# Packed attention, folded FFT and a two-layer block in seven products: two PSUM tiles instead of one, and down products dealt out between the block products

## The chip, the cores and the metric

The kernel runs on one core of a Trainium2 chip. The metric is device time in microseconds of one execution, as a median over runs. All data is float32.

## The reference

Attention is applied twice with a small set of packed tokens, then a Fourier mixing and a two-layer block:

```python
p_packed = sm_attn(p, k, v)            # B,H,S,D = 8,8,576,64; 32 packed tokens per head
x = sm_attn(q, p_packed, p_packed)     # softmax(scale * q k^T) v, scale = 1/8
x = x.transpose(0, 2, 1, 3).reshape(8, 576, 512)
u = x + np.real(np.fft.fft(np.fft.fft(x, axis=1), axis=2))
un = (u - mean(u)) / sqrt(var(u) + 1e-6)          # over the 512 features
return u + np.maximum(un @ w1, 0) @ w2            # w1 512 x 2048, w2 2048 x 512
```

## The kernel before

**Precision.** Every float32 operand of a large product is held as a high part and a low part (the remainder), both in a rounded format. One product is three matmuls: high·high, high·low, low·high. ScalarE makes a high part by a copy, VectorE or GpSimd the low part by a subtraction (helper `split`, lines 110 and 111).

**Rows and tiles.** The 8 × 576 rows of `u` are 36 groups of 128: four per batch and one of remainders per pair of batches. Four groups make a tile, so there are nine tiles of 512 rows, numbered 0 to 8. For each batch `front(b)` computes attention and the Fourier part and leaves rows of `u` in SBUF. It is a generator: the string ORDER lists its pieces, a `y` in it gives control back, and each call of `step(i)` in the block's code lets it run one stretch further. The front of batch t+1 is spread in this way over tile t. A tile's block (both layers) runs on TensorE between those pieces. The PSUM banks that a front uses come from `bank()`, which deals out a pool of two, and, in the first tiles, accumulators and `pb`.

**Order.** From tile 1 on TensorE, VectorE, ScalarE and GpSimd take their instructions in the order in which the code is written. SP's DMA queue is in order as well: a load that waits for its buffer holds up what is behind it.

**Plain form, tiles 0 and 1 (`ffn`).** There are 16 hidden blocks of 128. `up` makes one block's 512 columns in bank `ph` by 12 matmuls; ScalarE applies relu and VectorE forms the low part; `down` adds 12 matmuls into the accumulators `acc0` to `acc3`. In tile 1 `combine` (line 748 is its GpSimd part) writes, for each pair of hidden blocks, seven combinations of weights to DRAM, of 256 KB each.

**Seven-product form, tiles 2 to 8 (`fast_ffn`).** Two hidden blocks times two halves of the rows are four products of halves, and they are made from seven products instead of eight, eight times a tile; each of these eight is called a step here, m = 0 to 7. The right operands are B11, B21, B22 (quarters of the turned rows, in `uh` and `ul`) and the combinations T1 to T4 (in the tiles `fast`, the high parts in one and the low parts in another). One product is six matmuls of 128 × 256 (line 878), and goes to a half of one of the two PSUM banks `ph` and `pb`. These banks are one tile, `pair`. Four quarters come out as sums: B11 + B21, which collects in one half-bank and goes through relu at L899; `u2` = B11 + T2 (ScalarE copy L893, VectorE add L895); `u3` = `u2` + T3 + T1 (L906, L907), relu L909; and `u2` plus the half-bank that collects T1 and B22, beside `u2` plus that of T3 and T4, both in one 512-wide add (L919), relu L920. L884 makes the low parts on VectorE. Then 24 matmuls of 128 × 512, the downs (L936), add the two hidden blocks into the accumulators. The downs of step m−1 are all issued between T3 and B22 of step m:

```python
begin(m)            # B11, copy, T2, add, T1, B21, relu
step(4 * m - 2)     # a piece of the front
second(m)           # T3 and its sums; then 8 downs of m-1, step, 16 downs
end(m)              # B22, T4, the wide add; then step
```

After step 7 the tile's last 24 downs run at once, and `leave` (L944, L945) adds the accumulators to `u` and stores.

**Pieces and weights.** SP fetches the pieces (L762, one 256 KB piece per product) into a ring of eight slots, which lie in the space that `w1` had. A slot is fetched again as soon as its product has been issued. The `w2` rows are split once per hidden block and tile (L110, L111).

**Turning rows.** `Turned.less` normalises a row group of the next tile (L667), `moves` transposes it on TensorE by four 128 × 128 transposes into a bank (L676), and `parts` makes the high and low parts and T1 to T4 from it. Row groups 0 and 1 are turned in step 7, and 2 and 3 among the last 24 downs.

Of the kernel before, what the change touches and what calls it, by code (L numbers as in the profile page):

```python
# [17 lines left out]
P = 128  # L18
S = 576
# [33 lines left out]
RING = 8  # L53
# [29 lines left out]
def tile_kernel(ctx, tc, kpT, qT, v, w1, w2, tabs, tabR, tabB, tabT, sel, ident_d, out):  # L83
# [12 lines left out]
    pair = psf.tile([P, 2, 512], F32, tag="pair", name="pair")  # L96
    ph, pb = pair[:, 0, :], pair[:, 1, :]
# [556 lines left out]
    class Turned:  # L654
# [25 lines left out]
        def parts(self, i):  # L680
# [19 lines left out]
            nc.gpsimd.tensor_tensor(q[:, 1], raw[:, 2:4, w], r[:, 1], ALU.subtract)  # L700
# [3 lines left out]
            nc.scalar.copy(sh[:, 2:4], q)  # L704
            nc.gpsimd.tensor_tensor(sl[:, 2:4], q, sh[:, 2:4].bitcast(F32), ALU.subtract)
# [10 lines left out]
    def groups():  # L716

        if not fast:
            for i in range(3):
                fast[i] = work.tile([P, GROUPS[i + 1] - GROUPS[i], 512], F32R, tag=f"w1{i}", name=f"fast{i}", bufs=1)  # L720
        return fast

    def mixed():
        return [groups()[i][:, 0:4, :].rearrange("p i (k t) -> p i k t", k=2) for i in (1, 2)]

    def piece(n):
        i, a = ((1, 4), (1, 5), (2, 4), (2, 5), (0, 0), (0, 1), (0, 2), (0, 3))[n % RING]
# [53 lines left out]

    def ffn(first, turned, step, nxt):
# [41 lines left out]
        prev = None  # L824
        for j in range(NJ):
            last = nxt is not None and j == NJ - 1
            if last:
                cur = up(j, nxt.moves(0) + nxt.moves(1), lambda: less(2, 3))
                nxt.parts(0)
                nxt.parts(1)  # L830
            else:
                cur = up(j)
            next(splits, None)
            if nxt is not None and j == NJ - 2:
                less(0, 1)
# [344 lines left out]
```

## Time and profile before

| what | value |
|---|---|
| median of 2 runs | 1342.06 us (1339.34 to 1344.78) |
| the profiled execution | 1348.84 us |
| its span | 1347.0 us |
| its mean granted TensorE clock | 0.921 |
| moved to and from HBM over the span | 151.46 MB read, 24.12 MB written |

The span is from the first to the last instruction of one profiled execution; the run's own time is a little longer. The views used below are the totals by engine, the chain of work that ended last, the busy time of each engine in stretches of the span, instructions in order of time, and groups of equal instructions. In a row of the timeline stand the start in us, the duration, the engine, the line, the operation, what it writes and reads, and in brackets the idle time of that engine before it with the one who ended it. Names lose their numbers there: `fast` may be any of three tiles.

### The profile page before, as it was taken

What the parts mean: (1) busy time and instruction counts of PE and PEld (TensorE: products, weight loads), DVE (VectorE), ACT (ScalarE), POOL (GpSimd) and SP (SyncE); (2) the same over time, 40 slices, a digit from 0 to 9 for tenths busy, and PEclk for the clock granted to TensorE, in tenths of its full rate; (3) what the DMA queues carried; (4) which work ended last, traced back from release to release, by engine and by line L of the source; (5) the groups of instructions that cost most, each with busy time, mean ns of one, the idle gap of its engine ahead of it and who ended that gap; (6) DMA issues with size and microseconds to landing.
All of it is one profiled execution on the core that took longest, in us unless ns stands there. A gap on an engine that the chain in (4) does not pass through costs nothing.

```text
span 1347.0 us, 18423 instructions
## 1 busy us (share of the span) xinstructions
PE 1080.1 (80%) x6700; PEld 884.4 (66%) x6700; DVE 691.8 (51%) x1581; ACT 445.0 (33%) x960; POOL 391.9 (29%) x364
## 2 busy tenths in 40 slices
PE   3499897878687888788877988788887888887877
PEld 1466775657576766667665867677665866666666
DVE  5868544875437454654546453654546453234222
ACT  4675433333322233222422232223322342222121
POOL 4437343544421123211322142211312141212111
PEclk8699998889897999889998997799988999996999
DMA  9364014433554326433553335342543334444341
GB/s 349 110 230 132 0 55 157 135 110 125 159 182 123 110 90 212 131 103 102 180 174 97 113 107 180 117 117 81 178 137 97 113 123 139 117 125 126 112 139 63
DMA packets 89753, 176.77 MB, mean 131 GB/s; under 512 B 9206, under 2 KB 24384, under 8 KB 89664
## 3 DMA queue, kind: packets, MB, share of 16 engines
q1 hardware_dynamic: 88688, 174.17, 41.2%
q0 software_dynamic: 976, 1.44, 0.3%
q8 instruction: 53, 0.87, 0.3%
q14 instruction: 36, 0.29, 0.1%
HBM read 151.46 MB, written 24.12 MB: 130 GB/s over the span
## 4 chain that ended last, share of the span: by engine, by line
PE 47%; DVE 16%; ACT 5%; issue 3%; POOL 2%; DVEq 0%; ACTq 0%; POOLq 0%
PE pair L878 22%; PE acc L936 19%; DVE sums L919 2%; DVE hql L884 2%; DVE sums L895 2%; ACT hqh L920 1%; DVE ubuf L631 1%; DVE turned L469 1%; ACT sums L893 1%; DVE turned L473 1%; DVE ul L884 1%; ACT e L306 1%; POOL mixraw L700 1%; ACT uh L899 1%; ACT hqh L899 1%
## 5 line engine op out<-in xcount | busy, mean ns | idle before, releaser
L111 POOL TENSOR_TENSOR wr_l<-w2f,wr_h 128x512 fp32r<-128x512 f32 x144 | 197.3, 1373 | 577.4 <-ACT wr_h L110 508.7
L878 PE MATMUL pair<-fast,fast 128*128 128x256 f32 x1008 | 209.9, 316 | 88.8 <-DVE sums L895 38.4
L878 PEld LDWEIGHTS pair<-fast,fast 128*128 128x128 f32 x1008 | 163.4, 210 | 114.4 <-DVE sums L895 47.6
L878 PE MATMUL pair<-uh,fast 128*128 128x256 f32 x672 | 168.1, 310 | 48.2 <-DVE sums L919 46.3
L878 PEld LDWEIGHTS pair<-uh,fast 128*128 128x128 f32 x672 | 128.2, 210 | 63.4 <-DVE sums L919 53.3
L936 PE MATMUL acc<-wr_h,hqh 128*128 128x512 f32 x336 | 136.7, 407 | 5.3 <-ACT hqh L920 5.3
L936 PE MATMUL acc<-wr_h,hql 128*128 128x512 f32 x336 | 136.6, 407 | 0.0
L936 PE MATMUL acc<-wr_l,hqh 128*128 128x512 f32 x336 | 135.8, 404 | 0.0
L878 PE MATMUL pair<-fast 128*128 128x256 f32 x336 | 94.5, 320 | 31.1 <-ACT sums L893 10.0
L919 DVE TENSOR_TENSOR sums<-sums,pair 128x512 f32<-128x512 f32 x56 | 38.4, 686 | 155.6 <-PE pair L878 155.6
L878 PE MATMUL pair<-ul,fast 128*128 128x256 f32 x336 | 102.2, 304 | 2.8 <-DVE stat L232 2.3
L110 ACT CAST wr_h<-w2f 128x512 fp32r<-128x512 f32 x144 | 88.1, 616 | 38.5 <-PE acc L936 23.6
L920 ACT ACTIVATE hqh<-sums 128x512 fp32r<-128x512 f32 x56 | 35.4, 632 | 185.7 <-DVE sums L919 185.7
L878 PEld LDWEIGHTS pair<-fast 128*128 128x128 f32 x336 | 66.9, 213 | 42.2 <-ACT sums L893 11.8
L884 DVE SCALAR_TENSOR_TENSOR hql<-sums,hqh 128x512 fp32r<-128x512 f32 (+1 forms) x84 | 50.7, 604 | 57.2 <-ACT hqh L920 43.6
L936 PEld LDWEIGHTS acc<-wr_h,hqh 128*128 128x128 f32 x336 | 64.4, 192 | 22.0 <-ACT hqh L920 8.4
L936 PEld LDWEIGHTS acc<-wr_h,hql 128*128 128x128 f32 x336 | 63.7, 190 | 19.2 <-issue 4.2
L878 PEld LDWEIGHTS pair<-ul,fast 128*128 128x128 f32 x336 | 70.7, 211 | 5.9 <-DVE stat L232 3.3
L798 PE MATMUL pair<-uh,wr_h 128*128 128x512 f32 (+1 forms) x132 | 56.0, 424 | 23.2 <-DVE hql L804 8.4
L936 PEld LDWEIGHTS acc<-wr_l,hqh 128*128 128x128 f32 x336 | 64.2, 191 | 13.8
L111 POOL TENSOR_TENSOR wr_l<-w,wr_h 128x512 fp32r<-128x512 f32 x32 | 44.3, 1385 | 88.3 <-ACT wr_h L110 88.2
L814 PE MATMUL acc<-wr_h,hqh 128*128 128x512 f32 x128 | 52.8, 412 | 3.9 <-ACT wr_h L110 2.2
(338 smaller groups left out, 2338.9 us busy)
## 6 DMA issues: line engine op xcount, KB each, us to landing
fast<-mixed SPq DMA_DIRECT2D x392, 256.0 KB, 2.8
kp<-kpT SPq DMA_DIRECT2D x16, 608.0 KB, 4.9
out<-ubuf SPq DMA_DIRECT2D x36, 256.0 KB, 2.1
vt<-v SPq DMA_DIRECT2D x14, 640.0 KB, 4.8
wst<-w SPq DMA_DIRECT2D x17, 512.0 KB, 4.3
qt<-qT SPq DMA_DIRECT2D x14, 576.0 KB, 4.6
ubuf<-w SPq DMA_DIRECT2D x9, 512.0 KB, 4.3
mixed<-mix_h SPq DMA_DIRECT2D x8, 512.0 KB, 3.1
```

Source lines behind the costliest of these rows:

```text
L110: nc.scalar.copy(hi, src)
L111: (lo_eng or nc.vector).tensor_tensor(lo, src, hi.bitcast(F32), ALU.subtract)
L306: nc.scalar.activation(e1[:, w], sc[g][c], AF.Exp, bias=nb, scale=0.125, accum_out=sm2[:, c:c + 1])
L798: nc.tensor.matmul(ph[:, t], l[:, c * P:(c + 1) * P], r[:, c, t], start=(k == 0), stop=(k == 11))
L814: nc.tensor.matmul(acc[i], l[:, w], r, start=(j == 0 and k == 0), stop=(j == NJ - 1 and k == 2))
L878: nc.tensor.matmul(o, w[:, l, k * P:(k + 1) * P], r[x][:, k, :], start=first and n == 0, stop=n == 5, skip_group_check=not first)
L884: eng.scalar_tensor_tensor(l, x, 0.0, h.bitcast(F32), ALU.max, ALU.subtract)
L895: nc.vector.tensor_tensor(u2, u2, x[:, 1, 0], ALU.add)
L899: nc.scalar.activation(h, x[:, 0, 0], AF.Relu)
L919: nc.vector.tensor_tensor(raw, u2.unsqueeze(1).to_broadcast([P, 2, 256]), x[:, :, 1], ALU.add)
L920: nc.scalar.activation(h, raw, AF.Relu)
L936: todo.append((a, i, lambda x=x, w=w, i=i, at=at, k=k, a=a: nc.tensor.matmul(acc[i], x[:, at], w, start=m == 0 and a == 0 and k == 0, stop ...
```

## The change

**Two tiles.** `ph` and `pb` are two PSUM tiles of one bank each, where `pair` was one tile of two.

**Downs dealt out.** The downs stand in a list, `late`, and `run(n)` issues n of them. Step m issues B11 and T2 (`one`), 4 downs, T1, B21 and T3 (`two`), 4 + 6 downs, B22 and T4 (`three_four`), 10 downs. The list goes on across tiles: a tile's last 24 downs are issued in step 0 of the next tile, ordered by accumulator, with each `leave` behind its accumulator's last down. The plain form's last 12 go into tile 2 in the same way. The sum at the end of a step is two adds of 256 (L977, L978) instead of one of 512.

The lines of the block move: products are at L940 in the new file, downs at L998, the copy at L953, its add at L955, fetches at L800, splits at L113 and L114.

TensorE in one of the last steps of tile 8, before, from the last matmul of T2 to the first of T4 (`fast_2984` and `fast_2985` hold T1 to T4 and four ring slots, `fast_2983` the other four slots):

```order
L878 MATMUL pair<-fast_2984,fast_2985 128x256
L878 MATMUL pair<-fast_2984,fast_2983 128x256 [waits DMAHW7_49,DVE_49]
...
L878 MATMUL pair<-uh,fast_2983 128x256 [waits DMAHW0_49]
...
L878 MATMUL pair<-fast_2984,fast_2983 128x256 [waits DMAHW1_49,DVE_49]
...
L936 MATMUL acc_10423<-wr_h,uh 128x512
L936 MATMUL acc_10423<-wr_l,uh 128x512 [waits Pool_49]
...
L936 MATMUL acc_10426<-wr_h,ul 128x512
L878 MATMUL pair<-uh,fast_2983 128x256 [waits DMAHW2_49,DVE_49]
...
L878 MATMUL pair<-fast_2984 128x256 [waits DMAHW3_49]
```

Now, from the first matmul of T2 to the downs behind T4 (`fast_3103` is now a ring of two slots and a quarter of the hidden block):

```order
L940 MATMUL pb<-fast_3053 128x256 [waits DMAHW6_49,DVE_49]
...
L998 MATMUL acc_10525<-wr_h,uh 128x512 [waits Activation_49]
L998 MATMUL acc_10525<-wr_l,uh 128x512 [waits Pool_49]
...
L998 MATMUL acc_10526<-wr_h,uh 128x512
L940 MATMUL ph<-fast_3053,fast_3054 128x256 [waits DMAHW7_49,Activation_49]
...
L940 MATMUL ph<-uh,fast_3054 128x256 [waits DMAHW0_49]
...
L940 MATMUL pb<-fast_3053,fast_3103 128x256 [waits DMAHW1_49,DVE_49]
...
L998 MATMUL acc_10526<-wr_l,uh 128x512
...
L998 MATMUL acc_10525<-wr_l,fast_3103 128x512 [waits Pool_49]
L940 MATMUL ph<-uh,fast_3103 128x256 [waits DMAHW2_49,DVE_49]
...
L940 MATMUL pb<-fast_3053 128x256 [waits DMAHW3_49]
...
L998 MATMUL acc_10525<-wr_h,fast_3103 128x512
```

Before, T1 follows T2 directly and all 24 downs stand between T3 and B22. Now four downs stand between T2 and T1, ten between T3 and B22, and ten behind T4.

**Ring.** The ring has six slots instead of eight. The two that were given up hold the middle quarter (`quarter(m, 1)`) of odd steps; before, all steps used the same half of `hqh` and `hql` for it.

**Rows turned sooner.** Row groups 0 and 1 of the next tile are turned behind step 6, groups 2 and 3 in step 7 (the four downs behind T2, and the first four behind T3, carry their transposes). `parts` only copies raw rows; the high and low parts are made later by `mix` (T1 to T4) and `plain` (B11 and B21 in one 1024-wide subtraction, B22), with their low halves partly on GpSimd. GpSimd at the boundary of tiles 6 and 7 before:

```order
L699 TENSOR_TENSOR mixraw<-mixraw,raw 128x256 [waits DVE_49]
L700 TENSOR_TENSOR mixraw<-raw,mixraw 128x256
L705 TENSOR_TENSOR fast_2985<-mixraw,fast_2984 128x4x128 [waits PE_49,Activation_49]
L111 TENSOR_TENSOR wr_l<-w2f,wr_h 128x512 [waits Activation_49]
L699 TENSOR_TENSOR mixraw<-mixraw,raw 128x256 [waits DVE_49]
L700 TENSOR_TENSOR mixraw<-raw,mixraw 128x256
L705 TENSOR_TENSOR fast_2985<-mixraw,fast_2984 128x4x128 [waits Activation_49]
```

And now (`ul` is the low part of the turned rows, `raw` and `low` copies of them):

```order
L730 TENSOR_TENSOR mixq<-mixr,raw 128x256 [waits DVE_49,PE_49]
L731 TENSOR_TENSOR mixq<-raw,mixr 128x256
L114 TENSOR_TENSOR wr_l<-w2f,wr_h 128x512 [waits Activation_49]
L730 TENSOR_TENSOR mixq<-mixr,raw 128x256 [waits DVE_49,PE_49]
L731 TENSOR_TENSOR mixq<-raw,mixr 128x256
L114 TENSOR_TENSOR ul<-raw,uh 128x1024 [waits Activation_49]
L235 TENSOR_TENSOR stat<-stat,mhalf 128x1 [waits DVE_49]
L114 TENSOR_TENSOR fast_3054<-mixq,fast_3053 128x4x128 [waits Activation_49] x2
L114 TENSOR_TENSOR ul<-low,uh 128x512 [waits Activation_49]
L114 TENSOR_TENSOR wr_l<-w2f,wr_h 128x512 [waits Activation_49]
```

Each group's two subtractions into the combinations and the one into T3 and T4 are there as before, the latter later. New on this engine are the two into `ul`, 1024 and 512 wide, ahead of the next weight split.

**Fronts.** The front of batch 2 starts with tile 1; that of batch b ≥ 3 starts at step call 30 of the tile b−2 (`AHEAD`), not at the start of tile b−1. For b ≥ 2 the first scores are made in two parts (`scores_part`): the 64-column tail first, then 512 columns, with a `y` between them. SP's queue at the last front's loads of `v` and `q`, before:

```order
L245 DMA vt<-v 128x1280 [waits DMAHW4_49]
L762 DMA fast_2984<-mixed_98 128x512 [waits DMAHW5_49,PE_49]
L762 DMA fast_2984<-mixed_98 128x512 [waits DMAHW6_49,PE_49]
L762 DMA fast_2985<-mixed_98 128x512 [waits DMAHW7_49,PE_49]
L762 DMA fast_2985<-mixed_98 128x512 [waits DMAHW0_49,PE_49]
L245 DMA qt<-qT 128x1152 [waits DMAHW1_49,PE_49]
L762 DMA fast_2983<-mixed_98 128x512 [waits DMAHW2_49,PE_49]
L762 DMA fast_2983<-mixed_99 128x512 [waits DMAHW3_49,PE_49]
L245 DMA qt<-qT 128x1152 [waits DMAHW4_49,PE_49]
```

And now (L1006 are stores of the tile before, which ended later in the queue):

```order
L247 DMA vt<-v 128x1280
L1006 DMA out<-ubuf 128x512 [waits DMAHW4_49,DVE_49]
L1006 DMA out<-ubuf 128x512 [waits DMAHW5_49,DVE_49]
L800 DMA fast_3054<-mixed_98 128x512 [waits DMAHW6_49,PE_49]
L800 DMA fast_3103<-mixed_98 128x512 [waits DMAHW7_49,PE_49]
L247 DMA qt<-qT 128x1152 [waits DMAHW0_49,PE_49]
L1006 DMA out<-ubuf 128x512 [waits DMAHW1_49,DVE_49]
L1006 DMA out<-ubuf 128x512 [waits DMAHW2_49,DVE_49]
L800 DMA fast_3103<-mixed_98 128x512 [waits DMAHW3_49,PE_49]
L800 DMA fast_3053<-mixed_99 128x512 [waits DMAHW4_49,PE_49]
L247 DMA qt<-qT 128x1152 [waits DMAHW5_49]
L800 DMA fast_3053<-mixed_99 128x512 [waits DMAHW6_49,PE_49]
```

The two loads of `qt` stood three rows apart and now five, with two stores and two fetches of pieces between them.

The diff, cut to its core:

```diff
-RING = 8
+RING = 6
+AHEAD = 30
...
-    pair = psf.tile([P, 2, 512], F32, tag="pair", name="pair")
-    ph, pb = pair[:, 0, :], pair[:, 1, :]
+    ph, pb = (psf.tile([P, 512], F32, tag=n, name=n) for n in ("ph", "pb"))
...
             raw = extra("raw")
-            h, l = (x.rearrange("p (c t) -> p c t", t=256)[:, :, w] for x in (uh, ul))
             if i < 2:
-                split(h[:, 0:4], l[:, 0:4], tp)
                 nc.scalar.copy(raw[:, :, w], tp)
                 return
...
+            nc.scalar.copy(self.low[:, :, w], low)
             nc.vector.tensor_tensor(r[:, 1], low, r[:, 0], ALU.subtract)
-            nc.scalar.copy(sh[:, 0:2], r)
             nc.gpsimd.tensor_tensor(q[:, 0], r[:, 1], raw[:, 0:2, w], ALU.subtract)
             nc.gpsimd.tensor_tensor(q[:, 1], raw[:, 2:4, w], r[:, 1], ALU.subtract)
-            nc.scalar.copy(h[:, 4:6], low)
-            nc.vector.tensor_tensor(sl[:, 0:2], r, sh[:, 0:2].bitcast(F32), ALU.subtract)
-            nc.vector.tensor_tensor(l[:, 4:6], low, h[:, 4:6].bitcast(F32), ALU.subtract)
-            nc.scalar.copy(sh[:, 2:4], q)
-            nc.gpsimd.tensor_tensor(sl[:, 2:4], q, sh[:, 2:4].bitcast(F32), ALU.subtract)
+
+        def mix(self, i, c):
+            w = slice(i % 2 * P, i % 2 * P + P)
+            x = (self.r, self.q)[c][i]
+            h, l = (y[:, 2 * c:2 * c + 2, :, w] for y in mixed())
+            split(h, l, x, (nc.vector, nc.gpsimd)[c])
+
+        def plain(self, c):
+            h, l = (x.rearrange("p (c t) -> p c t", t=256)[:, (0, 4)[c]:(4, 6)[c]] for x in (uh, ul))
+            split(h, l, self.low if c else extra("raw"), nc.gpsimd)
...
+        def one(m):
+            u2 = sums[:, 2 * (m % 2) + 1]
+            product(x[0][:, 0], B11, True)
+            nc.scalar.copy(u2, x[0][:, 0])
+            product(x[1][:, 0], T2, True)
+            nc.vector.tensor_tensor(u2, u2, x[1][:, 0], ALU.add)
+
+        def two(m):
+            u3, u2 = sums[:, 2 * (m % 2)], sums[:, 2 * (m % 2) + 1]
+            product(x[0][:, 1], T1)
+            product(x[0][:, 0], B21)
+            product(x[1][:, 1], T3)
+            h, l = quarter(m, 0)
+            nc.scalar.activation(h, x[0][:, 0], AF.Relu)
+            nc.vector.tensor_tensor(u3, u2, x[1][:, 1], ALU.add)
+            nc.vector.tensor_tensor(u3, u3, x[0][:, 1], ALU.add)
...
+        def three_four(m):
+            product(x[0][:, 1], B22)
+            product(x[1][:, 1], T4)
...
+            nc.vector.tensor_tensor(raw[:, 0], u2, x[0][:, 1], ALU.add)
+            nc.vector.tensor_tensor(u2, u2, x[1][:, 1], ALU.add)
...
+        for m in range(M):
             last = nxt is not None and m == M - 1
+            if m:
+                late.extend(downs(m - 1))
+            if len(late) == NJ - 4:
+                run(4)
+            one(m)
+            run(4, nxt.moves(2) if last else ())
...
+            step(4 * m)
+            two(m)
...
+            run(4, nxt.moves(3) if last else ())
...
+            step(4 * m + 1)
+            run(6)
+            three_four(m)
...
+            step(4 * m + 2)
...
+                run(10)
...
+            step(4 * m + 3)
...
+        late.extend(downs(M - 1))
         if nxt is None:
-            while leaving:
-                leaving.pop(0)()
+            run(len(late))
...
+            at = 2 * NJ * t + i
+            if not running and fronts and at >= (0, 2 * NJ, 2 * NJ * (fronts[0] - 2) + AHEAD)[min(fronts[0], 3) - 1]:
+                running.append(front(fronts.pop(0)))
```

More of the change, by code (lines that the diff above doesn't have):

```diff
@@ L820, in less, with leave @@
                 nxt.less(k)
[L824 to L835, printed above, removed]
[L836 to L848 removed]
+        def leave(i):
+            key = keys[i]
             u = u_of[key]
@@ L852, in ffn @@
             free.append(place_of[key])
-    leaving = []
+        prev, fast = None, nxt.fast
+        for j in range(NJ):
+            last = j == NJ - 1
+            if last:
+                cur = up(j, nxt.moves(0) + nxt.moves(1), (lambda: None) if fast else lambda: less(2, 3))
+                nxt.parts(0)
+                nxt.parts(1)
+                if fast:
+                    less(2, 3)
+            else:
+                cur = up(j)
+            next(splits, None)
+            if j == NJ - 2:
+                less(0, 1)
+            step(2 * j)
+            if prev is not None:
+                if last and fast:
+                    nxt.plain(0)
+                    down(j - 1, *prev, [lambda: None] * 4 + nxt.moves(2) + nxt.moves(3))
+                    for i in (2, 3):
+                        nxt.parts(i)
+                        nxt.mix(i, 0)
+                    for i in (2, 3):
+                        nxt.mix(i, 1)
+                    nxt.plain(1)
+                else:
+                    down(j - 1, *prev, [lambda: None] * 8 + nxt.moves(2) if last else ())
+                    if last:
+                        nxt.parts(2)
+                next(splits, None)
+            step(2 * j + 1)
+            prev = cur
+        if fast:
+            vh, vl = ready.pop(0)
+            hh, hl = prev
+            for i in range(n):
+                w = slice(i * P, (i + 1) * P)
+                for k, (l, r) in enumerate(((hh, vh), (hh, vl), (hl, vh))):
+                    late.append((lambda l=l, r=r, i=i, w=w, k=k: nc.tensor.matmul(
+                        acc[i], l[:, w], r, start=False, stop=k == 2), (lambda i=i: leave(i)) if k == 2 else None))
+            return
+        down(NJ - 1, *prev, nxt.moves(3))
+        nxt.parts(3)
+        next(splits, None)
+        for i in range(n):
+            leave(i)
     def fast_ffn(first, turned, step, nxt):
@@ L955, in fast_ffn @@
         M = NJ // 2
[L956 to L974 removed]
+        for m in range(M):
+            last = nxt is not None and m == M - 1
+            if m:
[4 more added lines that the diff above has]
+            run(4, nxt.moves(2) if last else ())
+            if last:
+                nxt.parts(2)
+            step(4 * m)
+            two(m)
+            if not ready:
+                next(splits, None)
+            if last:
+                nxt.mix(2, 0)
+            run(4, nxt.moves(3) if last else ())
+            if last:
+                nxt.parts(3)
+                nxt.plain(0)
+                nxt.mix(3, 0)
+            step(4 * m + 1)
+            run(6)
+            three_four(m)
+            if last:
+                nxt.mix(2, 1)
+                nxt.mix(3, 1)
+                nxt.plain(1)
+            step(4 * m + 2)
+            if nxt is not None and m == M - 2:
@@ L1009, in fast_ffn @@
+            assert not late
+            if len(ready) < 2:
+                next(splits, None)
+            step(4 * m + 3)
+            if nxt is not None and m == M - 2:
+                nxt.less(2)
+                nxt.less(3)
+        late.extend(downs(M - 1))
         if nxt is None:
-            while leaving:
-                leaving.pop(0)()
+            run(len(late))
     keys = []
```

200 lines of the change are left out of this document (75 added, 125 removed), and 4 rows, old and new, of the table ORDER.

## The prediction

> **What bounds the kernel now.** I read the totals and the chain first, then the span by stages, and then one step of the loop in order of time.
>
> ```profile
> span 1347.0 us, 18423 instructions
> PE 1080.1 (80%) x6700; PEld 884.4 (66%) x6700; DVE 691.8 (51%) x1581; ACT 445.0 (33%) x960; POOL 391.9 (29%) x364
> PE 47%; DVE 16%; ACT 5%; issue 3%; POOL 2%; DVEq 0%; ACTq 0%; POOLq 0%
> ```
>
> TensorE is busy for four fifths of the span, but the chain runs through it for only 47%; 23% of the chain is VectorE, ScalarE and GpSimd, on which TensorE waits. So there is room below the present time. Where it lies the stages tell: columns are span, busy time of PE, PEld, DVE, ACT, POOL, granted clock, DMA share, GB/s. The first row is tile 1 in the plain form, then come tiles 2 to 8 in the seven-product form.
>
> ```profile
> 220.00:353.00 133.00, 107.26 (x568) 83.04 (x566) 87.43 (x166) 48.59 (x93) 67.64 (x51) 0.94 0.37 122
> 353.00:500.00 147.00, 119.97 (x781) 101.83 (x782) 72.92 (x185) 42.77 (x99) 30.08 (x27) 0.88 0.45 139
> 500.00:646.00 146.00, 119.43 (x804) 99.72 (x802) 78.86 (x199) 45.55 (x105) 36.01 (x33) 0.93 0.43 134
> 646.00:791.00 145.00, 118.09 (x804) 99.01 (x804) 77.81 (x196) 45.31 (x104) 35.75 (x33) 0.95 0.44 135
> 791.00:946.00 155.00, 128.97 (x811) 108.87 (x810) 79.67 (x200) 46.38 (x108) 37.16 (x35) 0.86 0.42 127
> 946.00:1093.00 147.00, 120.06 (x801) 100.58 (x800) 77.57 (x195) 45.02 (x103) 35.13 (x32) 0.93 0.41 125
> 1093.00:1219.00 126.00, 103.42 (x594) 85.70 (x592) 44.99 (x89) 32.09 (x68) 31.46 (x28) 1.00 0.43 129
> 1219.00:1347.00 128.00, 99.89 (x522) 82.85 (x522) 33.70 (x64) 24.07 (x50) 24.20 (x20) 0.92 0.37 112
> ```
>
> Tiles 7 and 8 carry no attention front, and even there VectorE is far from full. One of their steps, from copy to copy (a bracket is the idle time before the row and its releaser):
>
> ```profile
> 1266.12 0.37 ACT L893 COPY sums<-pair 128x256 f32<-128x256 f32 x1 [0.35 <-PE pair L878]
> 1266.54 0.98 PE L878 MATMUL pair<-fast,fast 128*128 128x256 f32 x6 [0.46 <-ACT sums L893]
> 1267.62 0.42 DVE L895 TENSOR_TENSOR sums<-sums,pair 128x256 f32<-128x256 f32 x1 [1.13 <-PE pair L878]
> 1268.10 0.98 PE L878 MATMUL pair<-fast,fast 128*128 128x256 f32 x6 [0.58 <-DVE sums L895]
> 1270.72 0.39 PE L878 MATMUL pair<-fast 128*128 128x256 f32 x1 [0.93 <-DVE ul L884]
> ...
> 1275.73 0.39 PE L936 MATMUL acc<-wr_h,hqh 128*128 128x512 f32 x1
> 1275.96 0.40 PE L936 MATMUL acc<-wr_l,hqh 128*128 128x512 f32 x1
> 1277.13 0.28 PE L878 MATMUL pair<-uh,fast 128*128 128x256 f32 x1
> 1277.24 0.28 PE L878 MATMUL pair<-ul,fast 128*128 128x256 f32 x1
> 1278.75 0.69 DVE L919 TENSOR_TENSOR sums<-sums,pair 128x512 f32<-128x512 f32 x1 [5.22 <-PE pair L878]
> 1279.49 0.39 PE L878 MATMUL pair<-uh,fast 128*128 128x256 f32 x1 [0.78 <-DVE sums L919]
> 1280.51 0.37 ACT L893 COPY sums<-pair 128x256 f32<-128x256 f32 x1 [0.35 <-PE pair L878]
> ```
>
> The step lasts 1280.51 − 1266.12 = 14.4 us. Matmuls start 0.117 us apart at 256 columns and 0.234 at 512, so its 42 product and 24 down matmuls need 42 × 0.117 + 24 × 0.234 = 10.5 us. The other 3.9 are four waits (0.46, 0.58, 0.93, 0.78), each with a pipeline's drain of some 0.3 behind it: product T2 waits for the copy, T1 for the add of `u2`, T3 for the low half of the first quarter, the next B11 for the wide add at L919. Each is a wait for a reader of the other bank or of what was just written, with no matmul left to run meanwhile.
>
> **The change, part by part.**
>
> *Two tiles and dealt downs, quiet steps.* T2 now writes another tile than the copy reads. Four downs (0.94 us) stand between T2 and T1: T2's sum is ready 0.3 + 0.42 after its last start, so L955 ends before T1 to T3 need it. Ten downs (2.34 us) stand between T3 and B22; the chain there is add, add, two low halves, some 0.3 + 4 × 0.45 = 2.1 us. Ten more stand between T4 and the next B11, over adds of 0.42 each. All four waits are covered, the tightest by 0.2 us. I take 10.6 us a step; the bounds are 10.5 and 14.4. That T3 now comes straight behind B21 costs nothing, since B21's reader (relu, ScalarE) touches the other tile.
>
> *Tiles 7 and 8.* Tile 7: 8 × 10.6 = 85, plus 6 for the tile boundary (below): 92 for 126. Tile 8: the same 85, the 24 downs of its last step (5.6), and 4 for start and end: 95 for 128.
>
> *Tiles 3 to 6.* Each has 804 matmuls, of which 8 × 66 = 528 are products and downs. From the code 104 of the rest are 256 to 258 wide (12.4 us at 0.119), 172 are transposes or 32-row matmuls that run several at once, some 4 us. Pure matmul time is 84.4 + 16.4 = 101 us, against 145 to 155. What stays on top:
>
> ```profile
> 698.10:719.50 21.40, 13.95 (x70) 11.96 (x70) 16.40 (x30) 5.16 (x12) 5.56 (x4) 0.89 0.33 95
> 719.50:735.80 16.30, 13.56 (x66) 11.48 (x66) 9.57 (x30) 4.28 (x10) 2.87 (x2) 0.83 0.39 105
> 735.80:750.90 15.10, 12.79 (x78) 11.10 (x78) 7.82 (x30) 4.83 (x12) 3.10 (x2) 1.00 0.43 131
> 717.98 0.39 PE L878 MATMUL pair<-uh,fast 128*128 128x256 f32 x1 [4.63 <-DVE sums L919]
> ```
>
> (1) Softmax steps. These three steps of tile 4 hold 33.8 us of VectorE work, against 33 of matmuls; in the new order they are steps 2 to 4, no lighter. VectorE is the bound there: 33.8 plus about seven handovers of 0.8 (as the 0.78 in the step above) makes 39.5, so 6.5 are lost, in two or three stalls of 1 to 2 us instead of one of 4.63. (2) Tile boundary.
>
> ```profile
> L748 POOL TENSOR_TENSOR w<-w,mix_h 128x1024 fp32r<-128x1024 f32 x8 | 20.0, 2496 | 0.0
> L676 PE MATMUL untp<-ident,un 128*128 128x128 f32 x16 | 4.4, 273 | 1.8 <-DVE un L667 1.8
> L705 POOL TENSOR_TENSOR fast<-mixraw,fast 128x512 fp32r<-128x512 f32 x2 | 2.6, 1290 | 1.5 <-ACT fast L704 1.5
> L700 POOL TENSOR_TENSOR mixraw<-raw,mixraw 128x256 f32<-128x256 f32 x2 | 1.9, 967 | 0.0
> ```
>
> GpSimd now makes the low halves of `uh` in one 1024-wide subtraction (2.5 us) behind four of 256 (up to 1.0 each) and a weight split (1.3, as any of 512); the next B11 needs it. Three more of 512 and another split follow. Counted from the transposes of the last pair, GpSimd is done about 2 us after TensorE gets there. With 1 to 2 us for the normalised rows (1.8 today), 0.7 for a transpose bank and 1 for scores, exponentials and their transposes, I take 6. (3) Loads.
>
> ```profile
> fast<-mixed SPq DMA_DIRECT2D x392, 256.0 KB, 2.8
> qt<-qT SPq DMA_DIRECT2D x14, 576.0 KB, 4.6
> w<-w SPq DMA_DIRECT2D x3, 512.0 KB, 13.4
> ```
>
> SP takes its queue in order. The second `qt` is now issued behind the fetch that T2 of step 1 frees, and its first use comes after eight downs and three products, 4 us later; it needs 4.6, or 1.5 us more than there is when transfers share the engines. The ring of six leaves a piece at least 10.6 − 3.8 = 6.8 us between the free slot and its use, against 2.8: hidden, with 1 us for bursts. (4) 3 for the sums and rows of steps 5 and 6, where a few waits on two PSUM banks show, and 1.5 for half-clock stretches. Together 6.5 + 6 + 2.5 + 4.5 = 19.5, so 120.5 a tile, bounds 108 (half of it) and 135 (VectorE's waits as today).
>
> The clock column reads 1.00 where no wait passes 0.93 us and 0.83 to 0.89 around the one of 4.63. The Trainium skill (TensorE: Matmul & The Clock Gate, Part 1) says the clock halves after an idle window of about 3.4 us and comes back after a busy one; the trace agrees, and by that rule the 1.5 us would be nothing.
>
> *Tile 2* starts with the plain form's last twelve downs and is otherwise like the others: 116 for 147.
>
> *Before tile 2.*
>
> ```profile
> L798 PE MATMUL pair<-uh,wr_h 128*128 128x512 f32 x54 | 23.7, 438 | 9.6 <-DVE yl L111 4.6 <-DVE hql L804 2.9 <-DVE s L428 1.0
> L422 PE MATMUL pair<-qt,ppT 64*32 64x512 f32 (+1 forms) x16 | 1.4, 414 | 1.2 <-DVE hql L804 1.2
> ```
>
> The front's readers of `pb` hold up `ph`, and the other way round, because both are one tile. Between 220 and 353 us such waits are 7 us; with two tiles some come back as waits on the readers themselves. I take 8 for both plain tiles, bounds 0 and 20: 345 for 353.
>
> **Sum.** 345 + 116 + 4 × 120.5 + 92 + 95 = 1130 us of span. The profiled execution itself took 1348.8, 1.8 over its span; the two runs' median is 1342.06, 6.8 less. So 1130 + 1.8 − 6.8 = 1125 us.
>
> **Rivals.**
>
> A. *VectorE keeps the front tiles where they are* (chance 0.13). TensorE gets its waits back in the steps with front work, because VectorE takes its instructions in order and the block's adds stand behind the front's. For it: 16.4 us in one step. Against: over a tile VectorE is busy only 78 of 145 us. Tiles 3 to 6 at 135, tile 2 at 130: 345 + 130 + 540 + 92 + 95 = 1202, as a run 1197.
>
> B. *GpSimd holds VectorE up* (0.08).
>
> ```profile
> 709.11 0.18 DVE L448 TENSOR_SCALAR d<-z 128x18 f32<-128x18 f32 x1
> 713.88 2.51 POOL L111 TENSOR_TENSOR wr_l<-w2f,wr_h 128x512 fp32r<-128x512 f32 x2
> 714.25 0.95 DVE L448 TENSOR_SCALAR d<-z 128x18 f32<-128x18 f32 x1
> ```
>
> The same 18-column instruction takes 0.18 us alone and 0.95 when GpSimd is at work. In shorter steps GpSimd's share rises and the boundary has 2.5 + 4 × 1.0 + 5 × 1.3 = 13 us of it in a row. If VectorE lost half of GpSimd's 36 us in each of five tiles with a front, and TensorE all of that, it would be 90 us more: 1215. But instructions that read PSUM, as the adds do, show no such stretching (0.42 throughout). The Trainium skill (SBUF — State Buffer, SBUF: two separate sides) calls it an exclusive lock on a shared port pair: the loser blocks fully; those rows agree.
>
> C. *Slower: the ring starves* (0.02). Six slots instead of eight, refilled by a queue that also waits for stores and front loads. With five products between, a piece that lands after 13 us holds products to 13 / 5 = 2.6 us, 56 of them 146 us a tile, today's time and more. Landing must rise from 2.8 to 13 us; 13.4 occurs, but only while the program's first loads fill all engines. At 15 us the seven tiles take 1176 and the run 1516.
>
> D. *More of the same* (0.07): the stalls of the front tiles halve; 1075.
>
> My forecast has the remaining 0.70. Its own range is 1090 to 1170; toward A and B, which together hold 0.21, I widen it to 1080 to 1195. About 2% is what a measurement of this kernel tells from no change; all but C lie far beyond it. Faster 0.96, same 0.02, slower 0.02.
>
> **What would show it.** Right: in the tiles without front, steps of 10.5 to 10.8 us with no wait for the block's sums; tiles 3 to 6 at 115 to 126 us with waits at the boundary and in steps 2 to 4; clock at 1.00 nearly throughout; pieces landing in under 5 us. Wrong: quiet steps above 11.5 us, TensorE waiting for DMA, or front tiles above 130.

## The result and the profile after

The changed kernel takes **1120.86 us** (median of 2 runs, 1118.54 to 1123.17), against 1342.06 before: a ratio of **0.8352**, 95% interval 0.8248 to 0.8456. Five later runs beside the experiments gave 1122.23 us and 0.835 (0.832 to 0.8379). The forecast was 1125.

The totals of the profiled execution's page:

```profile
span 1121.4 us, 18540 instructions
PE 990.4 (88%) x6700; PEld 830.4 (74%) x6700; DVE 694.3 (62%) x1609; ACT 444.7 (40%) x972; POOL 417.6 (37%) x378
```

TensorE has the same 6700 matmuls and is busy for 990 us instead of 1080, in part because more of them ran at the full clock (mean granted clock 0.969 against 0.921). VectorE and ScalarE do what they did; GpSimd is busy for 26 us more (417.6 against 391.9). The stages (span; busy time of PE, PEld, DVE, ACT, POOL; clock; DMA share; GB/s), from tile 2 on, cut at the first copy of each tile (three of the front tiles):

```profile
337.60:453.30 115.70, 105.08 (x776) 92.04 (x776) 77.30 (x197) 43.60 (x101) 35.62 (x33) 0.98 0.51 165
...
571.70:693.10 121.40, 110.48 (x807) 94.08 (x806) 79.44 (x202) 46.13 (x110) 39.54 (x36) 0.99 0.50 162
...
811.70:934.50 122.80, 111.03 (x785) 94.31 (x784) 79.05 (x200) 45.98 (x107) 39.42 (x36) 0.96 0.47 149
934.50:1027.60 93.10, 88.27 (x550) 78.24 (x549) 37.37 (x78) 28.11 (x59) 30.94 (x25) 0.99 0.55 170
1027.60:1121.40 93.80, 89.24 (x543) 78.83 (x542) 33.74 (x72) 22.70 (x49) 25.02 (x20) 0.99 0.52 163
```

Counted from first copy to first copy in both kernels, every tile from 2 on takes 24 to 36 us less (tile 8 to the end of the span), with a front or without. A step of tile 7 in order of time, from the start of T2 to the start of B22:

```profile
956.47 0.28 PE L940 MATMUL pb<-fast 128*128 128x256 f32 x1
956.72 0.37 ACT L953 COPY sums<-ph 128x256 f32<-128x256 f32 x1 [1.49 <-PE ph L940]
...
957.45 0.42 DVE L955 TENSOR_TENSOR sums<-sums,pb 128x256 f32<-128x256 f32 x1 [2.00 <-PE pb L940]
958.10 0.28 PE L940 MATMUL ph<-fast,fast 128*128 128x256 f32 x1
959.53 0.87 PE L940 MATMUL pb<-fast,fast 128*128 128x256 f32 x6
...
961.87 0.42 DVE L946 SCALAR_TENSOR_TENSOR hql<-sums,hqh 128x256 fp32r<-128x256 f32 x1 [0.15 <-ACT hqh L968]
962.57 0.28 PE L940 MATMUL ph<-uh,fast 128*128 128x256 f32 x1
```

No row of TensorE has a bracket. T2 starts at 956.47, before the copy of the other bank does at 956.72. T1 starts at 958.10 behind four downs; the copy, the reader of T1's own bank, ended at 957.09, and the add, for which it waited when both banks were one tile, at 957.87. T3 starts at 959.53. B22 starts at 962.57, ten downs later; the last low half ended at 962.29. From copy to copy it is 10.55 us. The largest waits of TensorE in the seven-product form over the whole span, first before and then after (us in total, times, longest):

```profile
PE pair L878 <- DVE sums L895: 46.6, 56, 2.0
PE pair L878 <- DVE sums L919: 46.3, 34, 4.6
PE pair L878 <- ACT sums L893: 38.6, 50, 6.8
PE pair L878 <- DVE hql L884: 15.0, 17, 0.9
PE pair L878 <- DVE ul L884: 12.6, 18, 0.9
```

```profile
PE pb L940 <- DVE sums L955: 10.2, 10, 1.3
PE untp L707 <- DVE un L698: 9.5, 6, 2.2
PE ph L940 <- POOL ul L114: 8.4, 7, 1.5
PE ph L940 <- DVE hql L946: 8.4, 5, 1.7
PE s2T L452 <- DMA qt<-qT: 7.5, 4, 2.5
```

The five waits of before came 175 times and took 159 us, without the drain behind each. The ones that remain come 4 to 10 times each, not once in every step.

### The profile page after: what moved, and what is told of

It is laid out like the page before. It is cut to its first block, busy times and chain, and to the rows that moved or that the text cites. A ratio compares the mean times of both kernels' runs of the same rounds, so it can differ in the third digit from the quotient of the medians.

```text
span 1121.4 us, 18540 instructions
## 1 busy us (share of the span) xinstructions
PE 990.4 (88%) x6700; PEld 830.4 (74%) x6700; DVE 694.3 (62%) x1609; ACT 444.7 (40%) x972; POOL 417.6 (37%) x378
## 4 chain that ended last, share of the span: by engine, by line
PE 54%; DVE 28%; ACT 5%; POOL 5%; DMA 4%; issue 3%; DVEq 0%; SPq 0%; POOLq 0%; ACTq 0%
PE acc L998 18%; PE ph L940 9%; PE pb L940 7%; PE ph L837 5%; PE acc L853 4%; DMA qt<-qT 2%; POOL ul L114 2%; DVE turned L499 2%; DVE turned L503 2%; DVE f L539 1%; PE untp L707 1%; DVE hql L946 1%; DVE eo L521 1%; DVE s L509 1%; PE po L391 1%
## 5 line engine op out<-in xcount | busy, mean ns | idle before, releaser
L114 POOL TENSOR_TENSOR wr_l<-w2f,wr_h 128x512 fp32r<-128x512 f32 x144 | 196.5, 1364 | 481.0 <-ACT wr_h L113 468.2
L940 PE MATMUL ph<-uh,fast 128*128 128x256 f32 x672 | 149.6, 285 | 10.7 <-DVE hql L946 8.4
L940 PE MATMUL pb<-fast,fast 128*128 128x256 f32 x670 | 130.7, 284 | 7.4 <-DVE sums L955 7.4
L940 PEld LDWEIGHTS ph<-uh,fast 128*128 128x128 f32 x672 | 116.7, 192 | 17.4 <-DVE hql L946 10.6
L940 PEld LDWEIGHTS pb<-fast,fast 128*128 128x128 f32 x670 | 103.9, 191 | 8.9 <-DVE sums L955 8.9
L940 PE MATMUL ph<-ul,fast 128*128 128x256 f32 x336 | 96.0, 286 | 8.4 <-POOL ul L114 8.4
L113 ACT CAST wr_h<-w2f 128x512 fp32r<-128x512 f32 x144 | 88.0, 611 | 11.3 <-PE ph L837 4.9
L998 PE MATMUL acc<-wr_h,hql 128*128 128x512 f32 x224 | 92.4, 413 | 0.0
L998 PE MATMUL acc<-wr_h,hqh 128*128 128x512 f32 x224 | 90.3, 403 | 0.0
L998 PE MATMUL acc<-wr_l,hqh 128*128 128x512 f32 x224 | 90.0, 402 | 0.0
L940 PE MATMUL pb<-fast 128*128 128x256 f32 x338 | 81.9, 284 | 8.0 <-ACT e L337 5.3
L998 PE MATMUL acc<-wr_h,fast 128*128 128x512 f32 x224 | 79.8, 402 | 0.0
L940 PEld LDWEIGHTS ph<-ul,fast 128*128 128x128 f32 x336 | 64.2, 191 | 13.7 <-POOL ul L114 10.4
L114 POOL TENSOR_TENSOR wr_l<-w,wr_h 128x512 fp32r<-128x512 f32 x32 | 44.6, 1396 | 79.7 <-ACT wr_h L113 79.7
L940 PEld LDWEIGHTS pb<-fast 128*128 128x128 f32 x338 | 60.3, 190 | 8.9 <-ACT e L337 5.5
L998 PEld LDWEIGHTS acc<-wr_h,hql 128*128 128x128 f32 x224 | 42.5, 190 | 14.2 <-issue 5.4
```

What stands on the lines that cost most here:

```text
L113: nc.scalar.copy(hi, src)
L114: (lo_eng or nc.vector).tensor_tensor(lo, src, hi.bitcast(F32), ALU.subtract)
L940: nc.tensor.matmul(o, w[:, l, k * P:(k + 1) * P], r[x][:, k, :], start=first and n == 0, stop=n == 5, skip_group_check=not first)
L998: nc.tensor.matmul(acc[i], y[:, at], w, start=first, stop=last),
```

## The experiments

The theory: a product waits for every reader of the tile that it writes. Two tiles take away the waits for readers of the other bank; downs in front of a product hide the others. Rival 1 says that the dealing carries the gain alone, rival 2 that the tiles do. Four kernels cross the two remedies. "Clumped" puts all 24 downs between T3 and B22, as before; in the changed kernel a tile's last 24 still go over into the next tile's step 0.

**One tile, downs dealt out.**

```diff
-    ph, pb = (psf.tile([P, 512], F32, tag=n, name=n) for n in ("ph", "pb"))
+    pair = psf.tile([P, 2, 512], F32, tag="pair", name="pair")
+    ph, pb = pair[:, 0, :], pair[:, 1, :]
```

> The changed kernel with its two banks made one tile again, downs still dealt out. My theory (a product waits for every reader of the tile it writes, unless downs stand in front): only T2's wait for the copy has no cover, 0.46 and a drain of 0.3, so quiet steps of 11.3 us instead of 10.55, 56 x 0.76 = 43 us, and some 10 us in the plain tiles: 1165 to 1180 us. Rival 1, the dealing carries the gain: quiet steps under 10.8, under 1135 us. Rival 2, the two tiles carry it: quiet steps above 13, above 1260 us.

Measured: 1197.64 us, ratio to before 0.8928 (0.889 to 0.8966). Quiet steps are 11.33 us, as worked out. The rest is over the range because the plain tiles lose much more than 10 us: tile 2 starts at 366.5 us instead of 337.7. TensorE's largest wait is the expected one, 52 times:

```profile
PE pair L941 <- ACT sums L954: 32.6, 52, 1.9
```

**Two tiles, downs clumped.** `run` is made to issue transposes beyond its n downs, and the counts become:

```diff
-            run(4, nxt.moves(2) if last else ())
+            run(0, nxt.moves(2) if last else ())
-            run(4, nxt.moves(3) if last else ())
+            run(8, nxt.moves(3) if last else ())
-            run(6)
+            run(16)
-                run(10)
+                run(0)
```

> The changed kernel with two tiles, but all 24 downs between T3 and B22 as before. My theory: in quiet steps no product writes a tile that is still being read, since a product on the other tile (0.7 us) stands between and a drain and an add take 0.72, so 10.6 us a step, tiles 7 and 8 at 93 to 96; in tiles with a front VectorE is late by more than one product covers, and each late add stops TensorE: 4 to 10 us a tile, 1140 to 1170 us in all. Rival 1, the dealing carries the gain: quiet steps above 12.5, above 1220 us. Rival 2, the two tiles carry all of it: 1117 to 1127 us, front tiles at 118 to 123.

Measured: 1202.83 us, ratio 0.8966 (0.8913 to 0.9019). Both rivals' numbers are missed, and mine too. Quiet steps are 11.36 us, not 10.6. ScalarE and T1 in tile 8, in order of time, show why:

```profile
1127.72 0.63 ACT L979 ACTIVATE fast<-sums 128x512 fp32r<-128x512 f32 x1 [5.56 <-DVE sums L978]
1128.26 0.60 ACT L113 CAST wr_h<-w2f 128x512 fp32r<-128x512 f32 x1
1128.77 0.36 ACT L953 COPY sums<-ph 128x256 f32<-128x256 f32 x1
1129.19 0.38 PE L940 MATMUL ph<-fast,fast 128*128 128x256 f32 x1 [0.47 <-ACT sums L953]
```

ScalarE takes the relu of step m, a weight split and the copy of step m+1 in this order. Without the ten downs behind T4, T1 reaches the copy while the split is still ahead of it. My step costs forgot what stands on the reader's own engine. Tiles 3 to 6 take 134 to 136 us: the load of `qt` is waited for 15.5 us in four tiles, `L955` 22.7 and the copy 14.4 in the whole span.

**One tile, clumped** (both edits).

> The changed kernel with one tile and all 24 downs between T3 and B22. My theory: three of the four waits return (T2 for the copy 0.46, T1 for the add 0.58, the next B11 for two adds of 0.42, each with a drain of 0.3); T3's does not, since it now stands ahead of the low half. Quiet steps of 13.3 us, 56 x 2.75 = 154 us, and 10 to 40 more in plain and front tiles: 1285 to 1320 us. A rival: ring, turning and the fronts' order carry part of the gain, then under 1260 us.

Measured: 1310.95 us, ratio 0.977 (0.9732 to 0.9808), within the range. Quiet steps are 13.43 us, with the three waits that were named (0.52, 0.58 and 0.97):

```profile
PE pair L941 <- DVE sums L956: 43.7, 38, 3.2
...
PE pair L941 <- DVE sums L979: 22.3, 23, 1.0
```

So all the rest of the change (T3 ahead of the low half, the carry across tiles, ring, turning, the fronts' order) brings about 30 us by itself (1341.16 before, beside it).

The changed kernel's own time in this table is from the last group of runs:

| us | downs clumped | downs dealt out |
|---|---|---|
| one tile | 1310.95 | 1197.64 |
| two tiles | 1202.83 | 1122.23 |

Either remedy alone takes 108 to 113 us off, both together 189: they hide partly the same waits, 33 us of them.

**The kernel before with two tiles alone.** `ph` and `pb` become two tiles there, `x` in `fast_ffn` the list of both, and the wide add two adds:

```diff
-            nc.vector.tensor_tensor(raw, u2.unsqueeze(1).to_broadcast([P, 2, 256]), x[:, :, 1], ALU.add)
+            nc.vector.tensor_tensor(raw[:, 0], u2, x[0][:, 1], ALU.add)
+            nc.vector.tensor_tensor(u2, u2, x[1][:, 1], ALU.add)
```

> The kernel before, with two tiles alone (the 512-wide add becomes two of 256). My theory: no wait is left in quiet steps, 10.7 us instead of 14.4, 56 x 3.7 = 207 us less; the tiles with a front keep some waits for late adds: 1140 to 1175 us. Rival 1, the dealing carries the gain: quiet steps above 12.5 and above 1250 us.

Measured: 1146.16 us, ratio 0.8554 (0.8512 to 0.8597), as the theory has it. Quiet steps are 10.91 us, and no row of TensorE in them has a bracket. In tile 8 the copy comes right behind the relu (1066.29 to 1066.92), since here the weight splits stand among the downs, and T1 can start right behind it (the copy ends at 1067.18):

```profile
1066.83 0.35 ACT L892 COPY sums<-ph 128x256 f32<-128x256 f32 x1
1067.24 0.38 PE L877 MATMUL ph<-fast 128*128 128x256 f32 x1
```

So the two tiles, in the order of before, bring 195 of some 219 us; everything else in the change brings the last 24, and without the two tiles it brings 143. "Everything else" is not harmless by itself: with two tiles and clumped downs it costs 57 us (1146.16 to 1202.83), where with one tile it gains 30, and dealing the downs out then takes 81 us off. So the 108 us for two tiles in the table hold for the order of the changed kernel; in the order of before they are 195. No run deals the downs out in the kernel before with nothing else changed.

The second group of runs asks for the sizes of the smaller terms.

**Loads written earlier.** In both of the last ORDER strings:

```diff
-j y S y y x0 y x1 p0 y p1 d0 y d1 y N
+j y S V0 V1 y y x0 y x1 p0 Q0 y p1 Q1 d0 y d1 y N
```

> The changed kernel with the loads of v and q of the fronts from batch 2 on written right behind the work that frees their buffers, so that in SP's queue the second q load stands ahead of the fetch it now stands behind. My theory: the scores' wait for that load (1.32, 2.16, 1.55, 2.52 us in tiles 3 to 6) is queue order, since its buffer is free 2 us before it is issued; the waits fall under 0.8, tiles 4 and 6 lose their half-clock stretch too (3 us each): 8 to 13 us less than the changed kernel, 1107 to 1114 us. Rival: the loads share the transfer engines with fetches and stores, an earlier issue lands no sooner: waits as now, 1117 to 1124 us.

Measured: 1113.42 us, ratio 0.8288 (0.8261 to 0.8316): the theory's number, 0.7 to 0.8% below the changed kernel. Tile 4, step 1, in the changed kernel and then here (SP's rows are issues):

```profile
586.17 1.04 SPq L800 DMA_DIRECT2D fast<-mixed  x2
587.26 1.27 SPq L247 DMA_DIRECT2D qt<-qT  x1
594.09 1.51 PE L452 MATMUL s2T<-qt,ppT 64*32 64x512 f32 x14 [2.16 <-DMA qt<-qT]
```

```profile
583.85 0.40 SPq L247 DMA_DIRECT2D qt<-qT  x1
584.50 9.17 SPq L800 DMA_DIRECT2D fast<-mixed  x7
589.22 1.09 PE L452 MATMUL s2T<-qt,ppT 64*32 64x512 f32 x16
```

The second load goes out before the fetches, and the wait is gone in all four tiles but for 0.16 us in tile 5. Tiles 3 to 6 take 116.6 to 117.3 us instead of 118.4 to 122.8: 1.4 to 5.6 us less for waits of 1.32 to 2.52. The step itself, both kernels:

```profile
586.20:605.10 18.90, 16.74 (x113) 12.48 (x111) 9.09 (x20) 4.79 (x11) 3.81 (x4) 0.91 0.64 210
```

```profile
584.50:598.60 14.10, 14.10 (x113) 11.48 (x112) 9.04 (x20) 4.72 (x10) 3.87 (x4) 1.00 0.80 281
```

It is 4.8 us shorter for a wait of 2.16; the other 2.6 are the same 113 matmuls, busy for 16.7 us at a mean clock of 0.91 and for 14.1 at 1.00.

**Low halves of the turned rows on VectorE.**

```diff
-            split(h, l, self.low if c else extra("raw"), nc.gpsimd)
+            split(h, l, self.low if c else extra("raw"), nc.vector)
```

> The changed kernel with the low halves of the turned rows (the 1024-wide subtraction and a 512-wide one) on VectorE instead of GpSimd. My theory: the 1.28 us that the next tile's B11 waits for them goes and VectorE has room at the boundary: 0.5 to 1.5 us less in each of seven tiles, 1110 to 1118 us. Rival B of the prediction in small (GpSimd's work holds VectorE up): 10 us less or more, with steps 7 and 0 shorter by over 1.5 us each. Rival, VectorE is the bound at the boundary: steps 7 longer, 1124 to 1135 us.

Measured: 1141.68 us, ratio 0.8493 (0.8461 to 0.8524): slower than the changed kernel, which no theory had. The boundary wait for GpSimd is gone, and the wait for `qt` grew from 7.5 to 18.0 us:

```profile
595.90 4.21 SPq L800 DMA_DIRECT2D fast<-mixed  x5
600.16 0.42 SPq L247 DMA_DIRECT2D qt<-qT  x1
```

In this kernel SP's order put the second load behind five fetches instead of two, 2.8 us later in the tile. The four steps with that wait (step 1 of tiles 3 to 6) take 86.5 us together instead of 71.6. SP's order isn't written out by hand, so an edit on another engine moved it. To see the edit without that, the two were combined below.

**A ring of four** (`RING = 4`, nothing else).

> The changed kernel with a ring of four slots instead of six. My theory: a slot freed by B11 is used again by T3, three products and four downs (3.0 us) later, against a landing of 2.8 behind the queue; the other six have 4.4 to 6.8 us. So T3 waits 0 to 0.8 us a step: 1125 to 1170 us. Rival C of the prediction (the ring is the bound): over 1250 us, with several products a step waiting. No wait at all (1117 to 1124) would say that six slots have much to spare.

Measured: 1126.62 us, ratio 0.8396 (0.8361 to 0.843), at the low end of my range. The waits for pieces that it adds are 13.2 us in all, eleven of them, one or two in each tile's steps 1 and 2, where the fronts' loads and the stores stand in the same queue:

```profile
PE pb L940 <- DMA fast<-mixed: 13.2, 11, 2.2
```

Six slots show no such wait. The time understates them, since two other waits became shorter here: that for `qt` fell from 7.5 to 0.4 us and that for low halves from 8.4 to 3.4. Rival C needed the ring to be the bound, and it isn't with four.

**No carry across tiles.** The last 24 downs are written at the tile's end:

```diff
         late.extend(downs(M - 1))
-        if nxt is None:
-            run(len(late))
+        run(len(late))
```

> The changed kernel with the last 24 downs of a tile issued at its end and not in the next tile's step 0. My theory: step 0 has no downs left as cover, so B22 waits for the sums of T3 (1.6 us) and the next B11 for its adds, and the tile's end waits for the last low half (1.4 us), while the wait for GpSimd at the boundary (1.28) goes: 1.5 to 3 us more in each of six tiles, 1128 to 1141 us. Rival: the boundary is ruled by GpSimd's chain, which 5.6 us of downs would hide: 1108 to 1117 us.

Measured: 1137.28 us, ratio 0.8465 (0.8436 to 0.8495), in the theory's range, but not by its way: TensorE doesn't take these downs at the tile's end. At the start of tile 4 the first copy, that of the next tile's B11, comes ahead of them, and T1 behind them:

```profile
576.73 0.38 ACT L953 COPY sums<-ph 128x256 f32<-128x256 f32 x1
577.84 0.50 PE L998 MATMUL acc<-wr_h,uh 128*128 128x512 f32 x1
585.49 0.28 PE L940 MATMUL ph<-fast 128*128 128x256 f32 x1
```

At tile 3 it is the same. So at these boundaries the order of the engine isn't that of the code, and the 24 downs stand in one piece between T2 and T1 of the next tile's step 0. The wait for GpSimd's `ul` stayed at 8.4 us, since it belongs to B11, ahead of those downs; the rival, that downs ahead of B11 would hide it, is not tested by this run. New are waits for a weight's low part (and 5.6 us more for low halves, 14.0 in all), while no wait for `qt` is left:

```profile
PE acc L998 <- POOL wr_l L114: 13.1, 6, 3.1
```

**Early loads with the low halves on VectorE, with another dealing, and with both.** The other dealing is 8, 8, 8 (`run(8)` behind T2, `run(4)` twice, `run(8)` behind T4). The changed kernel ran beside them.

> The changed kernel itself, beside the variants below on one chip: 1117 to 1125 us by every theory.

> The early loads of v and q, and the low halves of the turned rows on VectorE. My theory: VectorE alone made the boundary and the plain tiles shorter (tile 2 started 5.7 us sooner, tiles 7 and 8 took 0.7 and 1.3 less) and lost only through SP's queue, where the second q load had slid behind five fetches (issued at 600.2 in tile 4, after 8 us in which its buffer was free). With the load's place fixed the gains stay: 1098 to 1106 us. Rival, VectorE as bound at the boundary: 1113 us or more, steps 7 and 0 longer than in the early-load kernel.

> The early loads, and the downs dealt 8, 8, 8 instead of 4, 10, 10. My theory: what is left in steps 2 to 4 are products that wait for a late sum (T3 for the add of u2 0.73 and 1.31, B22 for a low half 1.68), and four more downs (0.94 us) ahead of T1 hide part of it: 2.2 us less in each of tiles 2 to 6, 1100 to 1106 us, quiet steps still 10.55. Rival, VectorE's total work bounds those steps: the waits move to B22 and the next B11 and steps 2 to 4 keep their length: 1110 to 1117 us.

> All three edits. If they add up as my theory has it: 1088 to 1098 us. If VectorE bounds both the boundary and steps 2 to 4: 1108 us or more.

| kernel | us | ratio to before, interval |
|---|---|---|
| changed kernel | 1122.23 | 0.835 (0.832 to 0.8379) |
| early loads, low halves on VectorE | 1117.89 | 0.8312 (0.8282 to 0.8342) |
| early loads, 8/8/8 | 1134.5 | 0.8446 (0.8414 to 0.8478) |
| all three edits | 1136.72 | 0.8454 (0.8424 to 0.8483) |

Three forecasts of mine missed; the rivals' 1113 us or more for the second kernel and 1108 or more for all three edits came out. With the load's place mended, the low halves on VectorE bring nothing over the early loads alone (1113.42 in the other group). In tile 4 the wait of 1.3 us for GpSimd goes, but step 7 grows from 17.15 to 18.14 us, with 12.6 us of VectorE work in it instead of 11.3, and step 1 from 14.14 to 15.01. Step 7 grows by 0.8 to 1.0 us in every tile from 2 to 6; step 1 doesn't in tiles 5 and 6, and step 0 is not longer, as the rival had it, but 0.3 to 0.7 us shorter in tiles 3 to 6. Waits for a weight's high part are new (5.1 us in all). The earlier start of tile 2 (331.1 us instead of 337.9) is given back there, where a product waits 7.0 us for a front's exponential (5.3 in the changed kernel). The 8/8/8 dealing did shorten steps 2 to 4 of tile 4, from 37.6 to 36.6 us instead of by 2.2, but eight downs behind T2 reach the second weight's low part sooner, and GpSimd isn't done with it (9.6 us of such waits against 0.8 in the changed kernel):

```profile
PE acc L998 <- POOL wr_l L114: 9.6, 7, 2.2
```

Steps 0 and 7 of tile 4 are 1.9 and 1.4 us longer than with the early loads alone. The lowest time measured is that of the changed kernel with the early loads: 0.8288 (0.8261 to 0.8316) against 0.835 (0.832 to 0.8379), a small difference between two groups of runs on two chips.

## Why the prediction was right

The mechanism came out as forecast: quiet steps without a wait, and what is left of waits at the boundary and in steps 2 to 4. The span was forecast as 1130 us and is 1121.4, and the sum came that near in part by luck, since errors met in it, as shown below. The last term was also off: the profiled execution lies 2.3 us above the median, not 6.8.

**Quiet steps** (10.6 forecast): 10.55. Tiles 7 and 8, forecast 92 and 95, took 93.1 and 93.8. The four waits of before are shown to be what the crossed kernels say: in quiet steps one tile costs T2's wait (11.33), one tile with clumped downs three waits (13.43). The cover that the prediction called the tightest has 0.85 us to spare, not 0.2: B22 needs only the low half that is read from its own bank, which ended at 961.72 in the step above (L946 on `ph`); the second is made from `sums`.

**Tiles 3 to 6** (120.5 forecast): 118.4, 121.4, 118.6 and 122.8, a mean of 120.3. The 19.5 us on top of pure matmul time were made up a little differently:

- *Softmax steps, 6.5.* Steps 2 to 4 of tile 4 last 37.5 us with 33.1 of VectorE work, against 39.5 forecast. All three waits of TensorE there (1.68, 0.73 and 1.31) are for VectorE, as argued, and 4.5 us are lost and not 6.5. That VectorE's total work is the bound isn't shown: it is busy for 88% of these steps, and the 8/8/8 dealing, with the same work, made them about 1 us shorter.

```profile
605.10:617.50 12.40, 10.52 (x64) 8.78 (x63) 11.14 (x24) 5.18 (x11) 4.95 (x4) 1.00 0.53 177
617.50:629.10 11.60, 10.87 (x69) 9.58 (x68) 10.37 (x35) 3.95 (x9) 2.01 (x2) 1.00 0.52 160
629.10:642.60 13.50, 12.19 (x80) 10.89 (x79) 11.57 (x34) 5.11 (x12) 4.79 (x3) 1.00 0.44 136
```

- *Boundary, 6.* In tile 4 it is 1.82 for the normalised rows, 0.79 for scores that wait for a transpose bank and 1.27 for GpSimd, as worked out from its queue:

```profile
688.73 2.83 POOL L114 TENSOR_TENSOR ul<-raw,uh 128x1024 fp32r<-128x1024 f32 x1
691.61 0.38 PE L940 MATMUL ph<-ul,fast 128*128 128x256 f32 x1 [1.27 <-POOL ul L114]
```

  GpSimd's 1.27 was forecast as about 2. With 0.95 for the statistics in step 6 the waits are 4.8 us, some 6 with a drain of 0.3 behind each.
- *Loads, 2.5, and half-clock stretches, 1.5.* The early loads show both together: 1.4 to 5.6 us a tile, 3.4 in the mean. Against the profile of one of the five later runs of the changed kernel, where the four waits are 1.06 to 1.60 us, it is 2.1 in the mean. The place was right, the second `qt` behind a fetch; in tile 4 the two transfers of `qt` took 5.8 and 6.7 us, where the median before was 4.6.
- *Sums and rows of steps 5 and 6, 3.* Only the 0.95 above was found, which is counted at the boundary. The terms that were found (4.5, 6 and 3.4) come to 14 us of the 19.3 on top of my 101; the other 5 stand in no row of waits, so the pure matmul time was taken too low or small gaps add up. That stays open.

**Tile 2** (116 forecast): 115.7.

**Before tile 2** (345 forecast, bounds 333 to 353): 337.6. Here the size was wrong, and two errors met. I took 8 us for the two tiles in the plain form. In the kernel before with two tiles alone tile 2's first copy comes at 321.3 us, 33 us sooner than the 354.6 of before, more than my bound of 20: in the plain form a matmul into `ph` also waited for the fronts' readers of `pb`, ScalarE's and VectorE's, and the other way round. Within the plain tiles of before, from 62 to 354.6 us, TensorE's waits across the two banks are eleven rows and 24.2 us, where I had counted 7 between 220 and 353. The five largest, 19.3 us:

```profile
PE pair L798 <- DVE yl L111: 4.6, 2, 4.4
PE pair L798 <- ACT e L306: 3.9, 2, 3.4
PE pair L249 <- DVE hql L804: 3.8, 3, 1.4
PE pair L463 <- DVE hql L804: 3.5, 1, 3.5
PE pair L798 <- ACT e1T L350: 3.5, 1, 3.5
```

In the kernel with two tiles alone none of the five is left. Fifteen waits with a drain of 0.3 us behind each would be some 29 of the 33 us, by estimate; the rest is not found. The other error goes the other way: the rest of the change costs 16.4 us there, which I had put at nothing. 34 more matmuls run ahead of tile 2 (4.3 us of busy time), since the front of batch 3 now begins there with its first scores, and most of the rest are waits that two tiles alone don't show: 5.3 us of a product for a front's exponential, 3.3 for the maximum of scores in the `pb` bank, 2.2 for `fh`, and 3.5 more for low halves. With one tile and clumped downs the same part costs 14.6 us (tile 2 starts at 369.2 instead of 354.6). From tile 2 to the end the changed kernel is 36.6 us shorter than the one with two tiles alone.

**The rivals.** A: VectorE is busy 79 us of 118 to 123 in tiles 3 to 6, and TensorE waits for the block's sums and low halves in steps 2 to 4 only. B: VectorE's busy time is 694 us against 692, so GpSimd didn't hold it up more; moving two of GpSimd's subtractions per tile to VectorE brought nothing. C: a ring of four still gives 1126.62. D: 1075 would have needed the stalls halved; even the early loads leave 1113.

## What to carry to other kernels

In this program two PSUM banks that are one tile made every writer of one wait for the readers of the other: split the tile first, for here that alone was worth 195 of some 219 us, and only then deal out independent matmuls for what is left. The two remedies hide the same waits, so the worth of one must be measured with the other in place, and an added cover counts only if the reader's own engine has nothing else queued ahead of it. When an edit on one engine changes the time, look at the DMA queue's order as well: here one load slid behind three more fetches, and four steps took 15 us longer. And look in the trace whether an edit did what it says: downs that were written at a tile's end ran in the middle of the next tile's first step.

## What the runs showed of the hardware

In the profile shown above a wait of 2.16 us in the middle of a step was followed by one stretch of 3.41 us at half clock (594.63 to 598.04 us, where 512-wide downs start 0.43 us apart instead of 0.23), and one of 2.52 us came with 6.83 us of it; waits of 1.32 and 1.55 us came with none. The length of the wait alone doesn't decide it. In the later profile of the changed kernel a wait of 1.60 us was followed by no such stretch, and one of 1.59 us by 3.41 us of it (595.41 to 598.82):

```profile
594.92 1.54 PE L452 MATMUL s2T<-qt,ppT 64*32 64x512 f32 x14 [1.59 <-DMA qt<-qT]
```

In the first two steps of tile 8 of the kernel before (1218.78 to 1251.74 us) the clock is 0.65 and 0.72, and no wait there is over 1.10 us; so the prediction's reading, 1.00 where no wait passes 0.93 us, holds for its three steps and is no rule. The Trainium skill (TensorE: Matmul & The Clock Gate, Part 1) has the clock halve after an idle window of about 3.4 us. The stretches have that window's length or twice it, but none of these waits is that long. By that rule alone the prediction's 1.5 us for such stretches would have been nothing; they are there. Such a wait costs more than it shows: the step was 4.8 us longer for 2.16 us, and 4.2 for 1.59 (18.33 against 14.10 with the early loads).
